# One kv head's output weights per layer as groups of 24 rows in a two-layer decode kernel

## The chip, the cores and the metric

The kernel runs on one core of a Trainium2 chip. The metric is the device time of one execution in microseconds. A run of the program takes 2570.9 us (median of three).

## The reference

Two layers of a decoder are applied twice to one token for each of two sequences: attention over a cache of 32,768 keys with 8 kv heads of 4 query heads each, then a gated feed-forward block. Both layers read the same caches and the same weights.

```
def _A_ref(x, k_cache, v_cache, wq, wo):         # B=2, D=512, Hq=32, Hkv=8, Sk=32768, Dh=128
    q = (x @ wq).reshape(B, 1, Hq, Dh)
    scores = einsum("bhqd,bhkd->bhqk", q, k) * Dh ** -0.5
    o = einsum("bhqk,bhkd->bhqd", softmax(scores), v)
    return o.reshape(B, 1, Hq * Dh) @ wo
def _B_ref(x, w_gate, w_up, w_down):             # 512 -> 1792 -> 512
    return (gelu(x @ w_gate) * (x @ w_up)) @ w_down

x = x + _A_ref(layernorm(x), ...)
x = x + _B_ref(layernorm(x), ...)
x = x + _A_ref(layernorm(x), ...)
x = x + _B_ref(layernorm(x), ...)
```

All values are float32. The output projection `wo` has 4096 rows of 512: 512 rows (1 MB) for each kv head, 128 for each of its 4 query heads.

## The kernel before

**Work and order.** A layer works through 16 pairs of a kv head and a sequence. For each pair it loads the keys in two pieces of 4 MB ([128 partitions x 16,384 numbers]) and the values in two such pieces. `scores` (L414) multiplies the keys, `softmax` follows, `values` (L485) multiplies the values, and `combine` (L494 to L503) brings the head's output `oT` into the form [128 rows of a head, 4 heads, 2 sequences]. After the second sequence of a kv head, `project` adds the head's share of the output projection to `W`, one bank of PSUM, in four groups of partitions. Layer 1 takes the pairs in the reverse order, so that the last keys and values of layer 0 are still there.

**Memory and queue.** All large data lie in one tile, `mem`, of 109 units of 512 numbers on each partition. A list, `stream`, has all loads in the order in which they are wanted. `pump` takes the next load when there is a hole of its size (a big piece has a slot of 32 units) and issues it on the SP queue (L199). `done` gives a slot back after the last product that reads it, and calls `pump` again; a load into it waits on SP until those products have run. Loads of 128 rows use 8 rows a DMA engine.

**The narrow loads.** For one kv head in each layer, (layer 0, head 6) and (layer 1, head 1), part of the output weights is stored in another form. `NARROW` has the number of query heads that are so stored: 2 in layer 0, 3 in layer 1. Their rows are cut into groups of 16 (`NROW`), and the groups lie beside each other on partitions 0 to 15, 8 groups (`NSEL`) for each query head. `pump` loads them in four transfers of four rows (L197): transfer i takes the partitions i, i+4, i+8 and i+12. They have a slot of 32 units to themselves. The other query heads of that kv head come in one more load of 128 rows, `("wo", l, g)`.

```
for i in range(4):
    nc.sync.dma_start(mem[i:NROW:4, c:c + cols], src[i])
```

**Projecting from the narrow form.** `narrow` needs the head's output in the same form. Eight small products with slices of the identity (L511) move the 16-row groups of `oT` to partitions 0 to 15 of a PSUM bank, one copy (L514) brings them to SBUF, and one product for each group and head (L519) adds to `W`. `project` then does the heads that were loaded wide (L529).

Of the kernel before, what the change touches and what calls it, by code (L numbers as in the profile page):

```python
# [16 lines left out]
P = 128  # L17
NB = 2
HKV = 8
REP = 4  # L20
DM = 512
# [6 lines left out]
HALF = 2048  # L28
# [31 lines left out]
WO_GROUPS = [[(0, 1), (2, 3), (4, 5), (6,), (7,)], [(7,), (6,), (5, 4), (3, 2), (1,), (0,)]]  # L60


NARROW = {(0, HKV - 2): 2, (1, 1): 3}
NROW = 16
NSEL = P // NROW


def pieces(split):

    out, s = [], 0  # L70
    for n in split:
        out.append((s, n))
        s += n
    return out


def parts(kind, l, pair):

    if kind == "k":
        return K_PARTS[l].get(pair, pieces(PLAIN))  # L80
    return pieces(V_SPLIT[l].get(pair, PLAIN))
# [51 lines left out]


@with_exitstack
def block_kernel(ctx: ExitStack, tc: tile.TileContext, x, consts, kt, vt, wq, wo, won, gu, wd, out):
    nc = tc.nc
    cp = ctx.enter_context(tc.tile_pool(name="cp", bufs=1))
    wk = ctx.enter_context(tc.tile_pool(name="wk", bufs=2))
# [4 lines left out]
    mem = cp.tile([P, UNITS * UNIT], F32, name="mem")  # L144
    holes = [(0, UNITS)]
    at = {}
# [3 lines left out]
    def take(key, n):  # L150
        if key in planned:
            o = planned[key]
            if not any(s <= o and o + n <= e for s, e in holes):
                return None
        elif n == CHUNK:
            spots = [o for o in range(0, UNITS - CHUNK + 1, CHUNK)
                     if any(s <= o and o + n <= e for s, e in holes)]
            if not spots:
                return None
            o = spots[0]  # L160
        else:
            fit = [(e - s, -s, e) for s, e in holes if e - s >= n]
            if not fit:
                return None
            size, s, e = min(fit)
            o = -s
        for i, (s, e) in enumerate(holes):
            if s <= o and o + n <= e:
                holes[i:i + 1] = [(x, y) for x, y in ((s, o), (o + n, e)) if y > x]
                return o  # L170
        return None

    def give(o, n):
        holes.append((o, o + n))
        holes.sort()
        i = 0
        while i + 1 < len(holes):
            if holes[i][1] == holes[i + 1][0]:
                holes[i:i + 2] = [(holes[i][0], holes[i + 1][1])]
            else:  # L180
                i += 1

    def pump():
        while stream:
            key, src, rows, cols = stream[0]
            n = CHUNK if rows == NROW else cols / UNIT if key in planned else -(-cols // UNIT)
            o = take(key, n)
            if o is None:
                return
            stream.popleft()  # L190
            c = int(o * UNIT)
            at[key] = (o, n), mem[:rows, c:c + cols]
            if rows == NROW:


                for i in range(4):
                    nc.sync.dma_start(mem[i:NROW:4, c:c + cols], src[i])  # L197
            else:
                nc.sync.dma_start(at[key][1], src)  # L199

    def flat_of(key):
        if key not in at:
            pump()
        return at[key][1]

    def get(key, a):
        return flat_of(key).rearrange("p (a c) -> p a c", a=int(a))

    def done(key, s=0, n=None):

        o, size = at[key][0]
        n = size if n is None else n
        if s + n == size:
            del at[key]
        give(o + s, n)
        pump()
# [3 lines left out]
    def flat(src, g, b, s, n):  # L220
        h, c = divmod(s, CHUNK)
        return src[b, g, h, :, c * UNIT:(c + n) * UNIT]

    def add(key, src, rows, cols):
        stream.append((key, src, rows, cols))

    def meets(l, n):

        return (l == 0 and n == len(ORDER) - 1), (l == 1 and n == 0)

    def wo_group(l, g):
        return next(t for t in WO_GROUPS[l] if g in t)

    for l in range(2):
        for i, (s, m) in enumerate(pieces(WQ_SPLIT[l])):
            add(("wq", l, i), wq[:, s * DM:(s + m) * DM], P, m * DM)
        for n, (g, b) in enumerate(orders[l]):
            second = meets(l, n)[1]
            vp = parts("v", l, (g, b))
            for s, m in parts("k", l, (g, b)):  # L240
                add(("k", l, g, b, s), flat(kt, g, b, s, m), P, m * UNIT)
            for s, m in [] if second else vp:
                if n % 2 == 1 and s == vp[1][0] and not meets(l, n)[0]:
                    group = wo_group(l, g)
                    o = g % 2 * HALF
                    if (l, g) in NARROW:
                        h = NARROW[l, g]
                        add(("won", l, g), won[l, :, :, :h * NSEL * DM], NROW, h * NSEL * DM)
                        add(("wo", l, g), wo[g // 2, :, o + h * DM:o + HALF], P, (REP - h) * DM)
                    elif len(group) == 2 and g == group[0]:  # L250
                        add(("wo", l, g), wo[g // 2], P, 2 * HALF)
                    elif len(group) == 1:
                        add(("wo", l, g), wo[g // 2, :, o:o + HALF], P, HALF)
                add(("v", l, g, b, s), flat(vt, g, b, s, m), P, m * UNIT)
            if meets(l, n)[0]:

                add(("wo", l, g), wo[g // 2, :, g % 2 * HALF:(g % 2 + 1) * HALF], P, HALF)
        for e in range(2):
            half_of = gu[e * P * FH:(e + 1) * P * FH].rearrange("(p c) -> p c", p=P)
            for j, (c, m) in enumerate(pieces(GU_SPLIT[l])):  # L260
                add(("gu", l, len(GU_SPLIT[l]) * e + j), half_of[:, c:c + m], P, m)
        for j, (o, m) in enumerate(pieces(WD_SPLIT[l])):
            add(("wd", l, j), wd[:, o * DM:(o + m) * DM], P, m * DM)
# [15 lines left out]
    nc.scalar.dma_start(xT, x)  # L279
    nc.scalar.dma_start(cst, consts)  # L280
    pump()
    ident = cst[:, C_ID:C_ID + P]

# [27 lines left out]
    def tiny(name):  # L311
        if name in once:
            return once[name]
        twice[name].reverse()
        return twice[name][1]
# [4 lines left out]
    W = ps.tile([P, 512], F32, name="W")  # L320
# [5 lines left out]
    def big():  # L326
        return wk.tile([P, 512], F32, name="big")[:, :]
# [9 lines left out]
    def small():  # L337

        u = 0 if state["full"] else state["next"]
        state["next"] = 1 - u  # L340
        return M[u]
# [163 lines left out]
    def narrow(l, g, oT, final):  # L505

        m = small()
        heads = NARROW[l, g]
        n = heads * NB
        for j in range(NSEL):  # L510
            nc.tensor.matmul(m[:NROW, n * j:n * j + n], ident[:, NROW * j:NROW * j + NROW],  # L511
                             oT[:, :heads, :].rearrange("p t b -> p (t b)"), start=True, stop=True)
        on = big()[:NROW, :NSEL * n]
        nc.vector.tensor_copy(on, m[:NROW, :NSEL * n])  # L514
        w = get(("won", l, g), NSEL * heads)
        for i in range(NSEL * heads):
            q = i % 4
            j, t = i % NSEL, i // NSEL
            nc.tensor.matmul(W[32 * q:32 * q + NB, :], on[:, n * j + NB * t:n * j + NB * t + NB], w[:, i, :],  # L519
                             start=False, stop=(final and q < heads and i + 4 >= NSEL * heads))  # L520
        done(("won", l, g))

    def project(l, g, oT, first, final):
        if (l, g) in NARROW:
            narrow(l, g, oT, final)
            h = NARROW[l, g]
            w = get(("wo", l, g), REP - h)
            for t in range(h, REP):
                nc.tensor.matmul(W[32 * t:32 * t + NB, :], oT[:, t, :], w[:, t - h, :], start=False, stop=final)  # L529
            done(("wo", l, g))  # L530
            return
        group = wo_group(l, g)
        key = "wo", l, group[0]
        w = get(key, REP * len(group))
        o = REP * (g - min(group))
        for t in range(REP):
            nc.tensor.matmul(W[32 * t:32 * t + NB, :], oT[:, t, :], w[:, o + t, :], start=first, stop=final)  # L537
        if g == group[-1]:
            done(key)
# [127 lines left out]
    for l in range(2):  # L667
        queries(l)
        stage(l, 0)
        for n, (g, b) in enumerate(orders[l]):  # L670
            if n % 2 == 0:
                oT = tiny("oT")
            p, linv = softmax(*scores(l, n, g, b))
# [16 lines left out]
    assert not stream  # L690


_INS = ["x", "consts", "kt", "vt", "wq", "wo", "won", "gu", "wd"]


def groups(x):
# [50 lines left out]
```

## Time and profile before

| | |
|---|---|
| median of 3 runs | 2570.9 us (2570.72 to 2571.05) |
| span of the profiled execution | 2568.7 us; its time outside the span is not recorded |
| PE busy | 1374.8 us (54%) |
| DVE, ACT, POOL busy | 143.6, 81.4, 2.4 us |
| DMA | 1104.81 MB, mean 430 GB/s |
| narrow loads | 4 of 128 KB (layer 0), 4 of 192 KB (layer 1) |
| wide rest of the same kv heads | 512 KB (layer 0), 256 KB (layer 1) |

The span runs from the first to the last instruction of the profiled execution. In rows of PE, "x" counts the instructions recorded; a float32 product is recorded as two. The DMA share of a stretch is the mean busy share of the core's 16 DMA engines; packets are booked where they start, so in a short stretch it may be a few hundredths too high or too low. PEclk is the granted share of the TensorE clock.

### The profile page before, as it was taken

The page shows a single profiled execution, that of the slowest core. Times are in us where ns is not written, and L with a number is a line of the kernel's source. Part 1 is how long each engine was busy: PE and PEld are TensorE (multiplying, and loading weights), DVE is VectorE, ACT ScalarE, POOL GpSimd, SP SyncE. Part 2 cuts the span into 40 slices and gives each one's busy share as a digit, 9 for nine tenths or more (in the row PEclk, how much of TensorE's full clock was granted, in tenths as well). Part 3 has the DMA queues.
Part 4 walks back from the last instruction along what each step waited for, and adds up shares of the span by engine and source line. Part 5 has one row for each costly group of instructions (what it writes and reads, how often), then busy time and mean ns, then how long its engine had stood idle before and what let it go on. Part 6 is the DMA issues. An engine that isn't in the chain of part 4 may idle for free.

```text
span 2568.7 us, 20340 instructions
## 1 busy us (share of the span) xinstructions
PE 1374.8 (54%) x9526; PEld 369.8 (14%) x9526; DVE 143.6 (6%) x483; ACT 81.4 (3%) x188; POOL 2.4 (0%) x8
## 2 busy tenths in 40 slices
PE   3545555545544554564686554454555544554657
PEld 1111111111111111111121111111111111111112
DVE  0000000000000000000011000000000000000001
ACT  0000000000000000000000000000000000000000
POOL 0000000000000000000000000000000000000000
PEclk8777777777777777777798677677776777777779
DMA  9999999999999999999999999999999999999998
GB/s 425 429 434 434 428 437 431 432 433 434 429 438 428 435 433 431 434 431 432 424 410 438 429 433 434 430 433 435 431 434 432 431 435 431 433 433 430 431 432 371
DMA packets 27507, 1104.81 MB, mean 430 GB/s; under 512 B 3200, under 2 KB 3456, under 8 KB 6912
## 3 DMA queue, kind: packets, MB, share of 16 engines
q1 hardware_dynamic: 27136, 1103.44, 99.6%
q8 instruction: 74, 1.21, 0.2%
q10 hardware_dynamic: 288, 0.08, 0.0%
q14 instruction: 9, 0.07, 0.0%
HBM read 1103.45 MB, written 0.07 MB: 430 GB/s over the span
## 4 chain that ended last, share of the span: by engine, by line
DMA 69%; PE 22%; another core or an unknown queue 8%; DVE 1%; issue 0%; ACT 0%; SPq 0%; POOL 0%; ACTq 0%; DVEq 0%
DMA mem<-in_vt 41%; DMA mem<-in_kt 24%; PE A L485 11%; PE S L414 9%; DMA aux<-in_consts 2%; DMA mem<-in_gu 1%; DMA mem<-in_wq 1%; DMA mem<-in_wd 0%; PE W L537 0%; PE M L498 0%; ACT big L494 0%; PE T L460 0%; PE W L519 0%; PE W L559 0%
## 5 line engine op out<-in xcount | busy, mean ns | idle before, releaser
L414 PE MATMUL S<-mem,aux 128*32 128x512 f32 x4032 | 575.5, 734 | 527.1 <-DMA mem<-in_kt 526.7
L485 PE MATMUL A<-mem,big 128*16 128x512 f32 x4096 | 584.7, 734 | 480.8 <-DMA mem<-in_vt 480.8
L414 PEld LDWEIGHTS S<-mem,aux 128*32 128x32 f32 x4032 | 144.9, 132 | 945.3 <-issue 508.2
L485 PEld LDWEIGHTS A<-mem,big 128*16 128x16 f32 x4096 | 122.6, 113 | 913.5 <-DMA mem<-in_vt 514.9
L417 DVE TENSOR_REDUCE aux<-S 128x1 f32<-128x512 f32 x63 | 43.6, 691 | 1110.1 <-PE S L414 1110.1
L457 ACT ACTIVATE big<-S,aux 128x512 f32<-128x512 f32 x63 | 42.7, 683 | 1187.1 <-DVE aux L453 1187.1
L460 PE MATMUL T<-aux,big 128*128 128x128 f32 x256 | 50.2, 342 | 39.0 <-ACT big L457 38.7
L503 DVE TENSOR_REDUCE aux<-M 128x4 f32<-128x64 f32 x32 | 7.2, 225 | 1103.4 <-PE M L498 1103.4
L494 ACT ACTIVATE big<-A,aux 128x512 f32<-128x512 f32 (+1 forms) x34 | 22.3, 661 | 1149.0 <-PE A L485 1149.0
L461 DVE COPY big<-T 128x512 f32<-128x512 f32 x64 | 43.8, 691 | 59.8 <-PE T L460 59.8
L460 PEld LDWEIGHTS T<-aux,big 128*128 128x128 f32 x256 | 35.8, 172 | 49.7 <-ACT big L457 49.5
L498 PE MATMUL M<-aux,big 128*128 128x128 f32 x128 | 21.3, 287 | 24.9 <-ACT big L494 24.9
L465 PE MATMUL M<-aux 128*128 128x4 f32 x64 | 17.2, 339 | 29.4 <-DVE aux L463 29.4
L449 PE MATMUL M<-aux 128*128 128x128 f32 x32 | 10.3, 323 | 34.5 <-DVE aux L447 34.5
L373 PE MATMUL M<-mem,aux 128*32 128x512 f32 x128 | 20.6, 690 | 4.4 <-DMA mem<-in_wq 3.9
L498 PEld LDWEIGHTS M<-aux,big 128*128 128x128 f32 x128 | 13.4, 140 | 53.2 <-ACT big L494 53.2
L465 PEld LDWEIGHTS M<-aux 128*128 128x128 f32 x64 | 14.4, 280 | 39.1 <-DVE aux L463 39.1
L537 PE MATMUL W<-mem,aux 128*2 128x512 f32 x96 | 12.5, 592 | 3.8 <-DVE aux L503 3.8
L333 PE MATMUL A<-aux 128*128 128x256 f32 (+2 forms) x42 | 14.3, 421 | 0.3 <-DVE aux L350 0.3
L449 PEld LDWEIGHTS M<-aux 128*128 128x128 f32 x32 | 4.2, 133 | 63.6 <-DVE aux L447 63.6
L359 PE MATMUL M<-aux 128*128 128x8 f32 x2 | 0.6, 356 | 23.2 <-DMA aux<-in_x 23.2
L457 ACT ACTIVATION_READ_ACCUMULATOR big<-S,aux 128x1 f32 x63 | 12.3, 196 | 0.0
(102 smaller groups left out, 188.8 us busy)
## 6 DMA issues: line engine op xcount, KB each, us to landing
mem<-in_gu SPq DMA_DIRECT2D x16, 896.0 KB, 24.5
mem<-in_wo SPq DMA_DIRECT2D x5, 2048.0 KB, 53.5
mem<-in_vt SPq DMA_DIRECT2D x2, 4096.0 KB, 42.2
mem<-in_kt SPq DMA_DIRECT2D x1, 7168.0 KB
mem<-in_wq SPq DMA_DIRECT2D x6, 1024.0 KB, 8.2
mem<-in_kt SPq DMA_DIRECT2D x1, 6144.0 KB
mem<-in_kt SPq DMA_DIRECT2D x5, 1024.0 KB, 8.7
mem<-in_kt SPq DMA_DIRECT2D x1, 4352.0 KB
```

The source lines that it names most:

```text
L333: nc.tensor.matmul(bank, ident[:, :bank.shape[0]], part.to_broadcast([P, n]), start=True, stop=True)
L373: nc.tensor.matmul(qp[32 * t:32 * t + 32, :], window(k, v), w[:, i - s, :], start=(i < 4), stop=(i >= 8 * KC - 4))
L414: nc.tensor.matmul(banks[u][32 * t:32 * t + 32, :], pad[:, PAD_Q - 4 * c:PAD_Q + 32 - 4 * c], w[:, j - s, :], start=(j == tile_of[0]), sto ...
L417: nc.vector.tensor_reduce(mx[:, u:u + 1], banks[u], axis=AX.X, op=OP.max)
L449: nc.tensor.transpose(m[:, :P], nm.to_broadcast([P, P]), ident)
L457: nc.scalar.activation(p[u], banks[u], AF.Exp, bias=bias, scale=SCALE, accum_out=ls[:, u:u + 1])
L460: nc.tensor.transpose(T[u][:, k * P:(k + 1) * P], p[u][:, k * P:(k + 1) * P], ident)
L461: nc.vector.tensor_copy(p[u], T[u])
L465: nc.tensor.matmul(m[:, :REP], both.to_broadcast([P, P]), same, start=True, stop=True)
L485: nc.tensor.matmul(A[32 * t:32 * t + 16, :], p[u][:, at_p:at_p + 16], w[:, QUAD * i + t, :], start=(j == 0), stop=(j == NU // QUAD - 1))
L494: nc.scalar.activation(md[:, i:i + 512 // n], A[:, i:i + 512 // n], AF.Copy, scale=linv)
L498: nc.tensor.transpose(m[:, c * P:(c + 1) * P], md[:, c * P:(c + 1) * P], ident)
```

## The change

Both kv heads' output weights are now stored narrow as a whole: all four query heads, in groups of 24 rows, 5 groups a head, on partitions 0 to 23. They come in four transfers of six rows of 40 KB (partitions i, i+4, ... i+20). Of each head's 128 rows, 5 x 24 = 120 are so covered; the last 8 rows of the four heads, 32 rows in all, come in one transfer of 32 rows of 2 KB, beside the others in the same slot. The loads of 128 rows for these two kv heads are gone.

In `narrow`, five products with slices of the identity select the groups, and four accumulating products with a zero-padded piece of the identity (`edge`, made by a memset and a copy) put the four heads' last 8 rows on partitions 0 to 31. Two copies bring both to SBUF. Then 20 narrow products and one with the 32 rest rows add to `W`.

```diff
-NARROW = {(0, HKV - 2): 2, (1, 1): 3}
-NROW = 16
+NARROW = [(0, HKV - 2), (1, 1)]
+NROW = 24
 NSEL = P // NROW
+NREST = P - NSEL * NROW
+NCOLS = REP * NSEL
+REST_Q = (REP - 1) * NREST
...
                 for i in range(4):
                     nc.sync.dma_start(mem[i:NROW:4, c:c + cols], src[i])
+                rest = mem[:REP * NREST, c + cols:c + cols + DM]
+                nc.sync.dma_start(rest, wor[key[1]])
+                at[key] += (rest,)
...
                     if (l, g) in NARROW:
-                        h = NARROW[l, g]
-                        add(("won", l, g), won[l, :, :, :h * NSEL * DM], NROW, h * NSEL * DM)
-                        add(("wo", l, g), wo[g // 2, :, o + h * DM:o + HALF], P, (REP - h) * DM)
+                        add(("won", l, g), won[l], NROW, NCOLS * DM)
...
     def narrow(l, g, oT, final):
         m = small()
-        heads = NARROW[l, g]
-        n = heads * NB
+        n = REP * NB
+        on = big()
+        edge = on[:, 64:64 + 2 * REST_Q + NREST]
+        nc.vector.memset(edge, 0.0)
+        nc.vector.tensor_copy(edge[:, REST_Q:REST_Q + NREST], ident[:, NSEL * NROW:])
+        heads = oT.rearrange("p t b -> p (t b)")
         for j in range(NSEL):
-            nc.tensor.matmul(m[:NROW, n * j:n * j + n], ident[:, NROW * j:NROW * j + NROW],
-                             oT[:, :heads, :].rearrange("p t b -> p (t b)"), start=True, stop=True)
-        on = big()[:NROW, :NSEL * n]
-        nc.vector.tensor_copy(on, m[:NROW, :NSEL * n])
-        w = get(("won", l, g), NSEL * heads)
-        for i in range(NSEL * heads):
+            nc.tensor.matmul(m[:NROW, n * j:n * j + n], ident[:, NROW * j:NROW * j + NROW], heads, start=True, stop=True)
+        k = REP * NREST
+        for t in range(REP):
+            c = REST_Q - NREST * t
+            nc.tensor.matmul(m[:k, n * NSEL:n * NSEL + NB], edge[:, c:c + k], oT[:, t, :],
+                             start=(t == 0), stop=(t == REP - 1))
+        nc.vector.tensor_copy(on[:NROW, :NSEL * n], m[:NROW, :NSEL * n])
+        nc.vector.tensor_copy(on[:k, NSEL * n:NSEL * n + NB], m[:k, n * NSEL:n * NSEL + NB])
+        w = get(("won", l, g), NCOLS)
+        for i in range(NCOLS):
             q = i % 4
-            j, t = i % NSEL, i // NSEL
-            nc.tensor.matmul(W[32 * q:32 * q + NB, :], on[:, n * j + NB * t:n * j + NB * t + NB], w[:, i, :],
-                             start=False, stop=(final and q < heads and i + 4 >= NSEL * heads))
+            t, j = divmod(i, NSEL)
+            nc.tensor.matmul(W[32 * q:32 * q + NB, :], on[:NROW, n * j + NB * t:n * j + NB * t + NB], w[:, i, :],
+                             start=False, stop=(final and 0 < q and i + 4 >= NCOLS))
+        nc.tensor.matmul(W[:NB, :], on[:k, NSEL * n:NSEL * n + NB], at["won", l, g][2], start=False, stop=final)
         done(("won", l, g))

     def project(l, g, oT, first, final):
         if (l, g) in NARROW:
             narrow(l, g, oT, final)
-            h = NARROW[l, g]
-            w = get(("wo", l, g), REP - h)
-            for t in range(h, REP):
-                nc.tensor.matmul(W[32 * t:32 * t + NB, :], oT[:, t, :], w[:, t - h, :], start=False, stop=final)
-            done(("wo", l, g))
             return
```

The weights are laid out for this on the host (`won`, and the new `wor` for the 32 rest rows).

More of the change, by code (lines that the diff above doesn't have):

```diff
@@ L135, in block_kernel @@
 @with_exitstack
-def block_kernel(ctx: ExitStack, tc: tile.TileContext, x, consts, kt, vt, wq, wo, won, gu, wd, out):
+def block_kernel(ctx: ExitStack, tc: tile.TileContext, x, consts, kt, vt, wq, wo, won, wor, gu, wd, out):
     nc = tc.nc
@@ L690, in block_kernel @@
     assert not stream
-_INS = ["x", "consts", "kt", "vt", "wq", "wo", "won", "gu", "wd"]
+_INS = ["x", "consts", "kt", "vt", "wq", "wo", "won", "wor", "gu", "wd"]
 def groups(x):
@@ L730 @@
         "wo": f(np.asarray(A_wo).reshape(HKV // 2, 2 * REP, P, DM).transpose(0, 2, 1, 3)).reshape(HKV // 2, P, 2 * HALF),
-        "won": f(np.asarray(A_wo).reshape(HKV, REP, NSEL, 4, 4, DM)[[g for _, g in NARROW]]
-                 .transpose(0, 4, 3, 1, 2, 5)).reshape(len(NARROW), 4, 4, REP * NSEL * DM),
+        "won": f(np.asarray(A_wo).reshape(HKV, REP, P, DM)[[g for _, g in NARROW], :, :NSEL * NROW]
+                 .reshape(len(NARROW), REP, NSEL, NROW // 4, 4, DM).transpose(0, 4, 3, 1, 2, 5))
+        .reshape(len(NARROW), 4, NROW // 4, NCOLS * DM),
+        "wor": f(np.asarray(A_wo).reshape(HKV, REP, P, DM)[[g for _, g in NARROW], :, NSEL * NROW:])
+        .reshape(len(NARROW), REP * NREST, DM),
         "gu": halves(np.asarray(B_w_gate), np.asarray(B_w_up)),
```

## The prediction

> **What bounds the kernel now.** I read the head of the page first, then the DMA queues, the chain, what PE waits for, and last the busy time in chosen stretches, because the change moves bytes between DMA engines and little else.
>
> ```profile
> span 2568.7 us, 20340 instructions
> DMA packets 27507, 1104.81 MB, mean 430 GB/s; under 512 B 3200, under 2 KB 3456, under 8 KB 6912
> q1 hardware_dynamic: 27136, 1103.44, 99.6%
> q8 instruction: 74, 1.21, 0.2%
> q10 hardware_dynamic: 288, 0.08, 0.0%
> DMA 69%; PE 22%; another core or an unknown queue 8%; DVE 1%; issue 0%; ACT 0%; SPq 0%; POOL 0%; ACTq 0%; DVEq 0%
> PE S L414 <- DMA mem<-in_kt: 526.7, 59, 11.2
> PE A L485 <- DMA mem<-in_vt: 480.8, 65, 15.7
> ```
>
> The data queue q1 holds the 16 DMA engines for 99.6% of the span: the kernel is one long load. PE waits for keys 59 times, 526.7 us in all, and for values 65 times, 480.8 us: about 8 us of slack at each tile. PE's 22% of the chain lies between a landing and the issue that it frees, with other tiles already queued behind; what counts is whether any DMA engine runs dry. The span is 2568.7 us; the runs' median is 2570.9, so 2.2 us lie around the span, which I keep. (The profiled execution has no other time of its own.)
>
> A transfer is done when its last engine is done, so the question is which engines are last. The stretches answer by their DMA share, where one sixteenth, 0.06, is one engine:
>
> ```profile
> core 0: us, PE busy (x) PEld busy (x) DVE busy (x) ACT busy (x) POOL busy (x), PEclk, DMA share, GB/s
> 800.00:1075.00 275.00, 136.80 (x933) 36.25 (x929) 12.13 (x40) 7.09 (x16) 0.00 (x0) 0.73 1.00 433
> 1284.00:1300.00 16.00, 11.62 (x102) 4.36 (x102) 2.70 (x14) 2.19 (x6) 0.55 (x1) 1.00 0.94 378
> 1286.50:1287.50 1.00, 0.82 (x7) 0.48 (x6) 0.00 (x0) 0.67 (x2) 0.00 (x0) 1.00 0.77 320
> 1287.50:1288.50 1.00, 0.91 (x24) 0.70 (x26) 0.30 (x2) 0.00 (x0) 0.00 (x0) 1.00 0.72 301
> 1288.50:1289.50 1.00, 0.95 (x22) 0.52 (x13) 0.00 (x0) 0.37 (x2) 0.00 (x0) 1.00 0.79 330
> 2557.00:2562.00 5.00, 4.00 (x28) 0.88 (x20) 1.99 (x5) 0.98 (x2) 0.00 (x0) 1.00 0.75 312
> 2562.00:2563.00 1.00, 1.00 (x6) 0.30 (x2) 0.00 (x0) 0.52 (x1) 0.00 (x0) 1.00 0.51 201
> 2563.00:2564.00 1.00, 1.00 (x26) 0.59 (x28) 0.00 (x0) 0.07 (x1) 0.00 (x0) 1.00 0.21 84
> 2564.00:2565.00 1.00, 1.00 (x47) 0.90 (x40) 0.00 (x0) 0.00 (x0) 0.00 (x0) 1.00 0.10 37
> 2565.00:2566.00 1.00, 0.70 (x20) 0.14 (x12) 0.16 (x1) 0.00 (x0) 0.00 (x0) 1.00 0.00 0
> ```
>
> In mid-stream all 16 are busy and move 433 GB/s, 27.1 KB/us each. At the change of layers (1286.5 to 1289.5) the share is 0.72 to 0.79: four engines have nothing left. From 2557 to 2562 it is 0.75: again four are done, some 5 us before the others, which drop out from 2562 on, one or two of them lasting until about 2565. So four engines are ahead of twelve at the end of each layer, and the last one or two set the end. A reason stands in the page: 74 instruction fetches take 0.2% of 16 engines' span, 0.002 x 16 x 2568.7 = 82 us of engine time, and engines without fetches get ahead.
>
> **Which engines a narrow transfer uses.** The count of small packets tells it.
>
> ```profile
> L197 SPq DMA_DIRECT2D mem<-in_won x8: 576/577/724, 1075.9 to 2330.1; - x8
> L199 SPq DMA_DIRECT2D mem<-in_kt x73: 327/328/457, 1.2 to 2448.9; - x73
> L199 SPq DMA_DIRECT2D mem<-in_vt x68: 327/328/426, 35.7 to 2485.4; - x68
> L199 SPq DMA_DIRECT2D mem<-in_gu x16: 327/328/429, 1263.2 to 2539.2; - x16
> L199 SPq DMA_DIRECT2D mem<-in_wo x11: 328/426/440, 111.2 to 2469.2; - x11
> L199 SPq DMA_DIRECT2D mem<-in_wq x10: 327/328/397, 0.7 to 1326.1; - x10
> L199 SPq DMA_DIRECT2D mem<-in_wd x9: 327/328/328, 1299.7 to 2550.1; - x9
> mem<-in_won SPq DMA_DIRECT2D x4, 192.0 KB
> mem<-in_won SPq DMA_DIRECT2D x4, 128.0 KB
> mem<-in_wo SPq DMA_DIRECT2D x1, 512.0 KB
> mem<-in_wo SPq DMA_DIRECT2D x1, 256.0 KB, 31.5
> ```
>
> The 288 packets of q10 are two transfers of 128 rows and 16 closing packets each. Of the 3200 packets under 512 B, 128 are the rows of x and 32 the closings on q10; 3040 remain for SP. Its 187 wide loads and the store of the result close on 16 engines each, 188 x 16 = 3008. That leaves 32 for eight narrow transfers: four each, one a row. So a four-row transfer runs on four engines, and a six-row one should run on six, closing with 48 packets; the two rest transfers stand for the two wide ones that go. After the change the count should be 3216.
>
> I call the four laden engines A, the two that six rows add B, the other ten C, and take A to stay among the six.
>
> [...]
>
> **Bytes per engine.** At 27.1 KB/us (433 GB/s over 16), in thousands of bytes, with 1 KB of the page being 1024 bytes:
> - Layer 0 before: an engine of A has four rows of 32 KB, 131.1 or 4.84 us, and every engine 32 KB of the 512 KB wide piece, 32.8 or 1.21 us.
> - Layer 1 before: A has four rows of 48 KB, 196.6 or 7.26 us, and every engine 16.4 or 0.60 us of the 256 KB piece.
> - After, in each layer: the six have four rows of 40 KB, 163.8 or 6.05 us, and every engine two rows of 2 KB of the rest, 4.1 or 0.15 us.
>
> So in layer 0 A gets 6.05 + 0.15 - 4.84 - 1.21 = +0.15 us, B +4.99, C -1.06. In layer 1 A gets -1.66, B +5.60, C -0.45. Over both, A and C lose 1.51 us and B gains 10.59. The sum of bytes stays, so the time can only come from who is last.
>
> **If B is two of the four early engines** (my forecast), B's load falls into their idle time: 3 us or more at the change of layers (idle from 1286.5, new work only after 1289.5) and 5 to 8 us at the end (2557 against 2562 to 2565). In layer 0 I take the last to be a fetching engine of C: gain 1.06 us, passed on whole, as the twelve never run dry there. If A were last, it would be a loss of 0.15; if B's lead were only the 3 us seen, B would be last by 2.0. In layer 1 A holds 7.26 us of narrow rows against 4.84 in layer 0, so the one or two that last to 2565 are most likely of A and get 1.66 us back, until C, which stops about 1 to 2 us sooner and gets back 0.45, is last instead. I take 0.9, between 0.45 and 1.66. Sum: 1.06 + 0.9 = 2.0 us; the bounds are 2.0 - 0.45 = 1.6 us slower and 1.06 + 1.66 = 2.7 us faster. The work after the last feed-forward weights follows the same engines and moves with them. 2570.9 - 2.0 = 2568.9.
>
> **What else changes, at nothing.**
>
> ```profile
> 1139.87 0.56 PE L511 MATMUL M<-aux 128*16 128x4 f32 x16 [0.32 <-DVE aux L503]
> 1140.46 0.18 DVE L514 COPY big<-M 16x32 f32<-16x32 f32 x1 [0.65 <-PE M L511]
> 1140.70 4.29 PE L519 MATMUL W<-mem,big 16*2 16x512 f32 x32 [0.27 <-DVE big L514]
> 1144.92 1.87 PE L529 MATMUL W<-mem,aux 128*2 128x512 f32 x4
> 2393.44 7.75 PE L519 MATMUL W<-mem,big 16*2 16x512 f32 x48 [0.29 <-DVE big L514]
> L300 DVE MEMSET aux<- 128x162 f32 x1 | 0.2, 193 | 0.0
> ```
>
> PE now selects with 8 products (16 records, 0.56 us) and works off 16 or 24 narrow columns (32 or 48 records, 4.29 or 7.75 us) and two or one wide ones. After: 5 + 4 selecting products, 18 records at 0.035, 0.63 us; 20 columns, 40 records at 0.134 to 0.161, 5.4 to 6.5 us; one rest column, 0.27 (two records at 0.134) to 1.87 us (all of L529). Layer 0: 0.56 + 4.29 + 1.87 = 6.7 becomes 6.3 to 9.0 us; layer 1: 48 records become 40, 1.3 us less at 0.161. DVE gets a memset (under the 0.19 us of the 128 x 162 one) and two more copies at 0.18 each, about 0.5 us; the second copy holds the first narrow product. Behind these on PE stand the next tile's scores, and SP waits for them to free space; both have the 8 us a tile of slack above, and transfers queue two deep. Without that cover it is -0.4 to +2.3 us in layer 0 and about -1 in layer 1. SP issues five transfers as before, in the same place; six rows against four at 0.58 us is within 0.1 us. The next value tile in that slot waits for five landings instead of four, all older than PE's reading of them, which it already waits for.
>
> **Rivals.**
> (1) *B is not among the four early engines, but carries fetches like the rest.* Then B gets 10.59 us on top of a full load: it would have ended between 2562 and 2565 and now ends between 2572.6 and 2575.6, against 2565: +7.6 to +10.6 us, 2578.5 to 2581.5, say 2579.9; it decides from the point where B's lead is under about 8 us. One such engine of the two is enough. If layer 0's share is partly taken up at the change of layers, it is 5.6 - 0.5 = +5.1 or more, 2576. For it: nothing in any view names an engine, and of twelve engines outside A four are early, so two picked at random are both early in 6 of 66 pairs. Against it: A was picked as the lowest rows and must have been ahead too, or its 12 us of narrow rows would have shown as a lone straggler much longer than 2 us; engines that share a burden are likely neighbours; and following the packet record of the trace from each packet's end to the next one's start, the fetches take turns on a fixed set of engines, and those without them are mostly the first to start at the launch, A among these. That speaks for B being free of fetches, though not surely.
> (2) *Six rows do not give six engines.* With three engines, two rows of every transfer each, it is 12.1 us a layer and 0.15 for the rest, against A's 6.05 and 7.86 before: +6.2, of which about 1 falls into A's distance from the last, and +4.4, so 2580.5. With rows split over all 16, every engine has 65.5, 2.42 us, against C's 1.21 and 0.60: +1.2 and up to +1.8, at most 2573.9. The count of four for four rows speaks against both.
> (3) *Much faster.* The idle engine time at the two ends is bounded: 16 x 0.06 x 16 = 15 us at 1284 to 1300, 16 x 0.25 x 5 = 20 at 2557 to 2562 and 16 x (0.49 + 0.79 + 0.90) = 35 from 2562 to 2565. All of it shared evenly gives 70 / 16 = 4.4 us, 0.17%, so a gain over 0.2% is nearly excluded.
>
> [...]
>
> **How the numbers follow.** Forecast case 0.69: 2568.2 to 2572.5 by its bounds, likeliest 2568.9. Rival 1 has 0.24; rival 2 has 0.04 with three engines and 0.01 with all 16; rival 3 has 0.02. A difference of 0.2% is 5.1 us, about what a measurement of this kernel can tell from no change: the forecast's 2.0 us, 0.08%, lies within it. So same 0.70, slower 0.28, faster 0.02. The range must reach into rival 1: from 2567.5 (the bound of 2.7 us, with a little for the clock's spread between runs) to 2580.0, its middle, which leaves out about 0.17.
>
> **What would show it.** Right: 3216 packets under 512 B; narrow issues of 240 KB; the DMA share at 1286.5 to 1289.5 up from 0.75 to nearer 0.9 (two engines idle, not four); at the end two engines out early instead of four, and the last out 2 us sooner. Wrong by rival 1: a share that falls towards 0.1 for several microseconds at the end of each layer, two engines working alone, and waits for values of 5 us more after each narrow transfer. Wrong by rival 2: another count of small packets. If PE's waits shrink by the amount the time grows, my cover for PE was gone.

## The result and the profile after

The changed kernel takes 2580.2 us (median of five runs, 2580.12 to 2580.45), the kernel before 2570.9 beside it (2570.72 to 2571.05): 9.3 us more, a ratio of 1.0036 with a 95% interval of 1.0024 to 1.0048. The forecast was 2568.9 and its range ended at 2580.0. Rival 1 had said 2579.9.

From the page of the changed kernel, its waits and its DMA issues:

```profile
span 2578.4 us, 20354 instructions
DMA packets 27347, 1104.81 MB, mean 428 GB/s; under 512 B 3216, under 2 KB 3472, under 8 KB 6736
q1 hardware_dynamic: 26976, 1103.44, 99.3%
q8 instruction: 74, 1.21, 0.2%
PE S L418 <- DMA mem<-in_kt: 531.2, 59, 12.0
PE A L489 <- DMA mem<-in_vt: 489.1, 66, 16.4
mem<-in_won SPq DMA_DIRECT2D x8, 240.0 KB
mem<-in_wor SPq DMA_DIRECT2D x2, 64.0 KB, 37.4
```

The bytes are the same, the fetches too (74). The small packets are 3216, as worked out for six engines. PE's waits for keys and values went from 1007.5 to 1020.3 us in all: PE waits longer, so PE is not where the time went. The DMA engines are busy for 99.3% instead of 99.6%: some of them stand idle longer. The stretches of the changed kernel at the change of layers and at the end say where (columns as before; 0.06 in the DMA share is one engine):

```profile
core 0: us, PE busy (x) PEld busy (x) DVE busy (x) ACT busy (x) POOL busy (x), PEclk, DMA share, GB/s
1289.00:1290.00 1.00, 1.00 (x7) 0.30 (x2) 0.00 (x0) 0.00 (x0) 0.00 (x0) 1.00 0.96 397
1290.00:1291.00 1.00, 0.61 (x5) 0.13 (x8) 0.00 (x0) 0.00 (x0) 0.00 (x0) 1.00 0.80 334
1291.00:1292.00 1.00, 1.00 (x10) 0.30 (x2) 0.00 (x0) 0.22 (x1) 0.00 (x0) 1.00 0.51 211
1292.00:1293.00 1.00, 0.82 (x7) 0.53 (x6) 0.00 (x0) 0.62 (x2) 0.00 (x0) 1.00 0.24 101
1293.00:1294.00 1.00, 0.91 (x27) 0.69 (x29) 0.30 (x2) 0.00 (x0) 0.00 (x0) 1.00 0.09 36
1294.00:1295.00 1.00, 0.91 (x22) 0.49 (x10) 0.00 (x0) 0.37 (x2) 0.00 (x0) 1.00 0.14 45
2557.00:2562.00 5.00, 2.84 (x25) 0.55 (x24) 1.57 (x4) 0.98 (x2) 0.00 (x0) 1.00 1.02 424
2564.00:2566.00 2.00, 1.48 (x10) 0.33 (x10) 0.00 (x0) 0.00 (x0) 0.00 (x0) 1.00 0.99 402
2566.00:2568.00 2.00, 1.48 (x10) 0.33 (x10) 0.04 (x1) 0.47 (x1) 0.00 (x0) 1.00 0.69 273
2568.00:2570.00 2.00, 1.20 (x8) 0.30 (x9) 1.53 (x4) 0.51 (x1) 0.00 (x0) 1.00 0.23 91
2570.00:2572.00 2.00, 2.00 (x12) 0.41 (x11) 0.42 (x1) 0.00 (x0) 0.00 (x0) 1.00 0.07 29
2572.00:2574.00 2.00, 2.00 (x42) 1.18 (x42) 0.00 (x0) 0.60 (x1) 0.00 (x0) 1.00 0.06 24
```

At the change of layers the kernel before had a share of 0.72 to 0.79 and then went on. Now the share falls through 0.80, 0.51 and 0.24 to 0.09 and 0.14. The end of the stream falls through 0.69 and 0.23 to 0.07 and 0.06: from 2570 to 2574 a single engine works and fifteen have nothing left. That is rival 1's picture, with one lone engine where it had named two. Its other sign is there too: PE's wait for the values that are queued behind the narrow rows is longer. These are the products that end it in layer 0, before and after (start, length and, in brackets, the wait ahead of it in us):

```profile
1128.87 9.21 PE L485 MATMUL A<-mem,big 128*16 128x512 f32 x64 [11.51 <-DMA mem<-in_vt]
1133.95 8.98 PE L489 MATMUL A<-mem,big 128*16 128x512 f32 x64 [15.76 <-DMA mem<-in_vt]
```

The wait grew by 4.3 us.

### The profile page after: what moved, and what is told of

Its sections match the earlier page's. It is cut to its first block, busy times and chain, and to the rows that moved or that the text cites. A ratio compares the mean times of both kernels' runs of the same rounds, so it can differ in the third digit from the quotient of the medians.

```text
span 2578.4 us, 20354 instructions
## 1 busy us (share of the span) xinstructions
PE 1371.2 (53%) x9528; PEld 372.0 (14%) x9528; DVE 144.4 (6%) x489; ACT 81.4 (3%) x188; POOL 2.4 (0%) x8
## 2 busy tenths in 40 slices
DMA packets 27347, 1104.81 MB, mean 428 GB/s; under 512 B 3216, under 2 KB 3472, under 8 KB 6736
## 3 DMA queue, kind: packets, MB, share of 16 engines
q1 hardware_dynamic: 26976, 1103.44, 99.3%
q8 instruction: 74, 1.21, 0.2%
## 4 chain that ended last, share of the span: by engine, by line
DMA 69%; PE 22%; another core or an unknown queue 8%; DVE 1%; ACT 0%; issue 0%; SPq 0%; POOL 0%; ACTq 0%; DVEq 0%
DMA mem<-in_vt 45%; DMA mem<-in_kt 20%; PE A L489 12%; PE S L418 8%; DMA aux<-in_consts 2%; DMA mem<-in_gu 1%; DMA mem<-in_wq 1%; DMA mem<-in_wd 0%; PE W L545 0%; PE M L502 0%; ACT big L498 0%; PE W L531 0%; PE T L464 0%; PE A L418 0%
## 5 line engine op out<-in xcount | busy, mean ns | idle before, releaser
L531 PE MATMUL W<-mem,big 24*2 24x512 f32 x80 | 13.3, 825 | 0.6 <-DVE big L525 0.6
```

## The experiments

**Theory 1**: some of the 16 DMA engines carry no instruction fetches and run ahead; the four laden engines and one of the two added ones are among them, the other added one carries fetches, and its bytes now set the end of both layers. **Theory 2**: the layout itself (more partitions, the rest transfer, one slot of five transfers) costs the time, whichever engines carry it. The test kernels are written like the changed one, with three numbers for each of the two narrow kv heads: rows of a transfer (so engines), transfers, and query heads in the narrow form. The changed kernel is (6, 4, 4) twice; the kernel before is (4, 4, 2) and (4, 4, 3). A diff of `NARROW` with three numbers shows how a test kernel differs from the changed one. The kernel before, run beside them, gave 2570.8 to 2570.9 us. The brackets behind a ratio are its 95% interval, about 0.1% or 2.5 us either way in most runs, so a difference of one or two microseconds is an indication and no more.

**Five rows instead of six, whole heads.**

```diff
-NARROW = {(0, HKV - 2): (6, 4, 4), (1, 1): (6, 4, 4)}
+NARROW = {(0, HKV - 2): (5, 4, 4), (1, 1): (5, 4, 4)}
```

> Both heads stored whole in groups of 20 rows, four transfers of five rows: five DMA engines with 196.6 thousand bytes each per layer (7.26 us) instead of six with 163.8 (6.05). Theory 1 (of the two engines that six rows add, one carries instruction fetches like the ten others and is last alone): if it is the sixth engine, five rows leave it out; the four get +1.4 us in layer 0 and -0.45 in layer 1 against the kernel before, so 2571.2 us (2570 to 2573). If it is the fifth, it now has 2.4 us more over both layers than with six rows: 2582.5 us. Theory 2 (the layout costs it: the rest transfer, the selecting products, the extra copies): as with six rows, 2579 to 2581 us.

Measured: 2572.8 us, ratio 1.0009 [0.9999, 1.0018]. One engine less takes away 7.4 of the 9.3 us, though five engines now carry the bytes of six and the layout is of the same kind (six groups of 20 rows a head in place of five of 24). Theory 2 falls. The time is 1.6 us above the middle that theory 1 gave, inside its range. Stretches of this kernel:

```profile
1286.00:1290.00 4.00, 3.73 (x50) 2.10 (x50) 0.30 (x2) 0.95 (x3) 0.00 (x0) 1.00 0.84 351
2560.00:2562.00 2.00, 1.13 (x7) 0.13 (x6) 1.50 (x4) 0.73 (x2) 0.00 (x0) 1.00 0.80 332
2564.00:2566.00 2.00, 2.00 (x30) 0.90 (x30) 0.00 (x0) 0.60 (x1) 0.00 (x0) 1.00 0.10 39
```

A share of 0.80 to 0.84 is 13 engines, three out early. With four rows it was four (0.75). So the fifth engine was an early one, and it has been put to use. With six rows no such step is left (0.96, 0.80, 0.51, 0.24 at the change of layers) and one engine stays at work alone: the sixth was not an early one.

**Eight rows.** No rest is left over; two more engines get rows.

```diff
-NARROW = {(0, HKV - 2): (6, 4, 4), (1, 1): (6, 4, 4)}
+NARROW = {(0, HKV - 2): (8, 4, 4), (1, 1): (8, 4, 4)}
```

> Both heads stored whole in groups of 32 rows, four transfers of eight rows: eight DMA engines with 131.1 thousand bytes each per layer (4.84 us), no rest rows, 16 columns. Theory 1: the added engines that carry fetches get 4.84 - 1.21 = 3.6 us in layer 0 and 4.84 - 0.60 = 4.2 in layer 1, 7.9 instead of 10.6 with six rows, so 2.7 us under the six-row kernel: 2577.5 us. Theory 2: no rest transfer, no padded identity, fewer products, so near or below the kernel before: 2569 to 2572 us.

Measured: 2576.5 us, ratio 1.0023 [1.0014, 1.0033], 1.0 below theory 1's middle. More partitions and fewer bytes an engine: faster than six rows by 3.7 us, as bytes on the sixth engine would have it. Two stretches of its end:

```profile
2566.00:2568.00 2.00, 1.44 (x9) 0.47 (x4) 1.23 (x4) 0.51 (x1) 0.00 (x0) 1.00 0.14 57
2568.00:2570.00 2.00, 2.00 (x11) 0.40 (x10) 0.20 (x1) 0.36 (x1) 0.00 (x0) 1.00 0.15 57
```

Here two engines (0.14, 0.15) last alone, not one: of the seventh and the eighth, one more carries fetches, by the share.

The packet records of the traces show the same directly. In mid-stream a packet starts 3 or 4 ns before the booked end of the packet ahead of it on its engine (14 or so behind a fetch), so the packets string into 16 chains, one for each engine. I take some 290 us around the narrow rows of layer 0 (840 to 1125; 830 to 1120 with five rows), a stretch in which few ends coincide. Each of these four traces has eight chains with one fetch of q8 each there and eight with none. (A packet of q14, 8 KB and 0.3 us, in the traces of four and of six rows on a laden chain, is not counted.) With four rows a transfer none of the four laden chains has a fetch; with five, none of the five; with six, one of the six; with eight, two of the eight.

**Only layer 0 changed.**

```diff
-NARROW = {(0, HKV - 2): (6, 4, 4), (1, 1): (6, 4, 4)}
+NARROW = {(0, HKV - 2): (6, 4, 4), (1, 1): (4, 4, 3)}
```

> The change in layer 0 alone; layer 1 as in the kernel before. Theory 1: the one late engine costs its 4.99 us less its distance from the last engine in layer 0, and layer 1 adds nothing: 2574.5 us (2573 to 2576). Theory 2: about half of the 9.3 us too, 2575.5. If the loss arises in layer 1 alone (the narrow rows there stand close to the end): 2570 us.

Measured: 2576.2 us, ratio 1.0019 [1.001, 1.0029]. Layer 0 costs 5.4 us (2.6 to 7.5 by the interval), which leaves about 4.0 for layer 1. Stretches of this kernel at the two ends:

```profile
1292.00:1293.00 1.00, 0.82 (x6) 0.57 (x6) 0.00 (x0) 0.58 (x2) 0.00 (x0) 1.00 0.24 101
1293.00:1294.00 1.00, 0.91 (x27) 0.70 (x29) 0.30 (x2) 0.00 (x0) 0.00 (x0) 1.00 0.11 43
2564.00:2566.00 2.00, 1.23 (x8) 0.33 (x9) 1.51 (x4) 0.51 (x1) 0.00 (x0) 1.00 0.76 317
2566.00:2568.00 2.00, 2.00 (x12) 0.38 (x11) 0.42 (x1) 0.00 (x0) 0.00 (x0) 1.00 0.73 302
```

The lone engine stands at the change of layers alone; the end has the kernel before's 0.75 again, 5 us later.

**Six rows with half the load.** Two query heads narrow, two wide, in both layers.

```diff
-NARROW = {(0, HKV - 2): (6, 4, 4), (1, 1): (6, 4, 4)}
+NARROW = {(0, HKV - 2): (6, 4, 2), (1, 1): (6, 4, 2)}
```

> The changed kernel's transfers of six rows in both layers, but with two of the four query heads in the narrow form (rows of 20 KB instead of 40 KB), the other two as a load of 128 rows. Theory 1 (one of the two added engines carries instruction fetches, and its bytes set the end of both layers): it gets 81.9 + 32.8 + 2.0 = 116.8 thousand bytes a layer instead of 167.9, 1.89 us less at 27.1 KB/us, in each of two layers: 2580.2 - 3.8 = 2576.4, between 2575.5 and 2577.5. Theory 2 (six rows on 24 partitions cost a fixed time, whatever their length): 2579.5 to 2580.5.

Measured: 2576.0 us, ratio 1.002 [1.0011, 1.0029]. The time follows the bytes on the added engine: 4.2 us less for 3.8 worked out. A fixed price of six rows is out.

**No narrow loads at all.**

```diff
-NARROW = {(0, HKV - 2): 2, (1, 1): 3}
+NARROW = {}
```

> No narrow loads: both kv heads' output weights as loads of 128 rows like all the others. Every engine gets 65.5 thousand bytes a layer. Theory 1: the twelve get 32.8 (layer 0) and 49.2 (layer 1) more, 1.2 and 1.8 us: 2570.8 + 3.0 = 2573.8 where one of the twelve was last in both layers; 2572 where a laden engine was last in layer 1, which loses 5.4 us of load. Eight engines, not four, should then be out early at the end of a layer: a DMA share near 0.5 for some microseconds.

Measured: 2573.5 us, ratio 1.0011 [1.0002, 1.0021]. Stretches of this kernel:

```profile
1288.00:1289.00 1.00, 0.86 (x6) 0.67 (x6) 0.02 (x1) 0.45 (x2) 0.00 (x0) 1.00 0.57 238
1289.00:1290.00 1.00, 0.91 (x30) 0.71 (x32) 0.28 (x2) 0.00 (x0) 0.00 (x0) 1.00 0.50 208
1290.00:1291.00 1.00, 0.90 (x16) 0.49 (x8) 0.00 (x0) 0.37 (x2) 0.00 (x0) 1.00 0.52 215
2560.00:2562.00 2.00, 1.54 (x11) 0.16 (x7) 1.14 (x3) 0.93 (x2) 0.00 (x0) 1.00 0.53 222
2562.00:2564.00 2.00, 1.47 (x11) 0.58 (x12) 0.85 (x2) 0.05 (x1) 0.00 (x0) 1.00 0.50 207
```

With equal loads, half the engines are done early: eight of 16, for some 3 us at the change of layers and at least 4 at the end. So the order is: eight early with no narrow load, four with four rows, three with five.

**More instructions, no more data.** Is it the instruction fetches that the other eight carry?

```diff
+    def extra(bank, n):
+        for _ in range(28 if 0 < n < len(ORDER) - 2 else 0):
+            nc.tensor.matmul(bank[:16, :REP], ident[:, :16], same, start=True, stop=True)
...
         m = small()
+        extra(m, n)
         nc.tensor.transpose(m[:, :P], nm.to_broadcast([P, P]), ident)
```

(The same call stands ahead of the sum's product in `softmax` and of the transposes in `combine`.)

> The kernel before with 2184 small products more on TensorE (28 before each of three products of a pair, of 16 x 4 results each, in 26 of the 32 pairs, written over by the product behind them), so more instructions to fetch and no more data: 8736 instructions, where 20340 go with 74 + 9 fetches, about 34 fetches more. Theory 1 (eight of the 16 engines carry the fetches, those without them get ahead by as much, and the others set the end): 34 fetches at 1.1 us (82 us over 74) over eight engines, +4.7 us, 2575.5, between 2573.5 and 2578; the share of 0.75 before the end of a layer lasts longer by 2 to 3 us. Theory 5 (the lead of the early engines has nothing to do with fetches): the products stand in the slack of 8 us a tile, 2 us each, 2570.5 to 2571.5.

Measured: 2576.6 us, ratio 1.0023 [1.0013, 1.0032]. From its page and its stretches:

```profile
span 2574.7 us, 29076 instructions
q8 instruction: 108, 1.77, 0.3%
2564.00:2566.00 2.00, 1.22 (x7) 0.13 (x6) 1.41 (x4) 0.82 (x2) 0.00 (x0) 1.00 0.75 312
2566.00:2568.00 2.00, 1.79 (x12) 0.58 (x12) 0.58 (x2) 0.00 (x0) 0.00 (x0) 1.00 0.56 233
2568.00:2570.00 2.00, 2.00 (x30) 0.81 (x26) 0.00 (x0) 0.60 (x1) 0.00 (x0) 1.00 0.44 175
```

34 fetches more (108 for 74), 0.56 MB, cost 5.6 us: over eight engines 4.25 each, 1.3 us apiece where 1.1 was worked out. In the packet records the 108 fetches took 115.2 us together and the 74 before 79.0, which is 4.5 us more for each of eight engines; what the last 1.1 us are is not shown. The stretch of 0.75 did not get longer, as was expected. In its place the share falls on to about a half (0.56, 0.44) towards the end, as it would if the lead had outgrown what the four laden ones carry. Theory 5 falls: the lead comes from fetches. In mid-stream (800 to 1075 us) the share is 1.00, so the products hid in PE's slack. The 8736 instructions more stand against 34 fetches more, 257 apiece: PE has the slack for them, but this kernel, which its DMA engines bound, pays 5.6 us for the fetches.

**Six transfers of four rows** (groups of 24 rows, but on four engines, partitions i, i+6, i+12, i+18).

```diff
-NARROW = {(0, HKV - 2): (6, 4, 4), (1, 1): (6, 4, 4)}
+NARROW = {(0, HKV - 2): (4, 6, 4), (1, 1): (4, 6, 4)}
```

> The six-row kernel's layout (groups of 24 rows, 32 rest rows, the same products and copies), but loaded by six transfers of four rows: four DMA engines with 245.8 thousand bytes each per layer (9.07 us). Theory 1: the fifth and sixth engine are relieved; the four get 9.07 + 0.15 - 6.05 = +3.2 us in layer 0 and +1.4 in layer 1 against the kernel before, of which about 1 falls into their distance from the last in layer 0: 2574.5 us (2572.5 to 2575.5). Theory 2: the layout is as it was, 2579 to 2581 us.

Measured: 2592.5 us, ratio 1.0083 [1.0066, 1.0099]. Both theories missed it by over 11 us. Two things could be behind it: four engines with 246 thousand bytes each, or the step of six. With a step of four, and if the kth row goes to the kth engine, each engine writes to a group of four partitions of its own (4k to 4k+3); with a step of six, neighbours write into one another's group. Two kernels tell these apart.

**The kernel before with the rows of a transfer on adjacent partitions.**

```diff
-                    nc.sync.dma_start(mem[i:rows:parts_n, c:c + cols], src[i])
+                    nc.sync.dma_start(mem[r * i:r * i + r, c:c + cols], src[i])
```

> The kernel before, but each transfer of four rows goes to four adjacent partitions instead of every fourth one: the same bytes on the same four engines, with four engines writing into adjacent partitions at once. Theory 3 (the six transfers of four rows with their step of six lost time because several engines wrote into the partitions of one another): slower than before by some us to tens of us, 2574 to 2600. Theory 4 (they lost it because four engines with 246 thousand bytes each are overladen): nothing changes, 2570.8, between 2570.3 and 2571.5.

Measured: 2583.0 us, ratio 1.0049 [1.0034, 1.0064]. Apart from the partitions only the order of the rows in DRAM has changed, so that each partition gets the numbers that it had, and 12.1 us are lost. By the packet records the 16 narrow rows of 32 KB in layer 0 took 1.91 us each in the median and 3.07 at most, where all took 1.21 to 1.22 before; the 16 rows of 48 KB in layer 1 took 3.35 in the median, before 1.82. The load of 128 rows behind the narrow one in layer 1 lands 42.3 us after its issue, where it was 31.5 in the kernel before:

```profile
mem<-in_wo SPq DMA_DIRECT2D x1, 256.0 KB, 42.3
```

**Four engines with more bytes, each on its own partitions.**

```diff
-NARROW = {(0, HKV - 2): (6, 4, 4), (1, 1): (6, 4, 4)}
+NARROW = {(0, HKV - 2): (4, 4, 4), (1, 1): (4, 4, 4)}
```

> The kernel before, but with all four query heads narrow in both layers: the 16-row groups and transfers of four rows of 64 KB to every fourth partition, no wide rest. The four engines get 262.1 thousand bytes a layer, 9.68 us, against 6.05 (layer 0) and 7.86 (layer 1): more than in the kernel with six transfers of four rows (245.8 and 4.1), but each engine writes to its own partitions. Theory 3 (the partitions): +1.8 to +5 us, 2572.5 to 2576. Theory 4 (four overladen engines): like the six transfers of four rows, 2591 to 2595.

Measured: 2576.4 us, ratio 1.0023 [1.0013, 1.0032], just above theory 3's upper end. So 262 thousand bytes on each of four engines cost 5.6 us and not 22: theory 4 falls, and the partitions are shown to matter. The four engines of the six transfers are not the only ones to pay: around the narrow rows of that trace (1085 to 1150 and 2340 to 2420 us) 70 of 815 packets of 64 KB took over 3 us, where in the changed kernel 4 of 910 did and the median is 2.42. How the other 16 us come about in full stays open, and no run shows what makes the adjacent rows 12.1 us slower.

**A version that might beat both:** five engines, with the loads adjusted to their lead.

```diff
-NARROW = {(0, HKV - 2): (6, 4, 4), (1, 1): (6, 4, 4)}
+NARROW = {(0, HKV - 2): (5, 4, 3), (1, 1): (5, 4, 4)}
```

> Groups of 20 rows in transfers of five rows, with three query heads narrow in layer 0 and four in layer 1: five engines that are all early by theory 1 get 122.9 + 16.4 thousand bytes (layer 0) and 163.8 (layer 1), beside a rest load, and the others 16.4 less than before in each layer. Theory 1: a little faster than the kernel before, 2570.0, between 2569.5 and 2571.5, less than a measurement can tell. Theory 2 (narrow rows on more than 16 partitions cost a fixed time): 2572.5 or more, like the whole heads in transfers of five rows (2572.8).

Measured: 2571.6 us, ratio 1.0003 [0.9994, 1.0011]: no difference that can be told from the kernel before, and 1.6 us more than worked out. No version here beats the kernel before.

## Why the prediction was wrong

- *The bound* was right: DMA engines, and the last of them. In the kernel before, a load of 128 rows has eight packets and a closing one on each of 16 chains, and the products on the keys at 1069.29 us started 0.13 us after the last of its 16 closings had landed. The time came from idle engines at the two ends of layers, with the same bytes and mid-stream rate (433 GB/s from 800 to 1075 us before and after).
- *Six rows use six engines*: right (3216 small packets, on the number, and six chains). Rival 2 is out. The number alone does not set the time: with whole heads narrow, five engines took 2572.8 us, six 2580.2 and eight 2576.5. It hangs on which engines the rows go to.
- *B is two of the four early engines*: this is the step that failed. One of the two is early, the other carries fetches: with five rows 2572.8, with six 2580.2, and one fetch on one of the six chains. I had followed the packet records of the kernel before, and rightly found that the fetches take turns on a fixed set of engines, but only its four laden engines can be told by their rows there. The four laden engines are free of q8's fetches, as I took them to be, but I went on from them to "engines that share a burden are likely neighbours", a guess that no run shows. Nor does one show that A is among the six, which the sums take for granted: the runs show how many laden chains have a fetch (none of four, none of five, one of six, two of eight), and no view names an engine. The count that stood beside it, 6 of 66 pairs, was the better guide. It could have been sharpened: if four of twelve are early, two picked at random are both early in 9%, one of them in 48% (32 of 66 pairs), and rival 1 needs no more than one fetching engine.
- *Rival 1's sum* was right: +7.6 to +10.6 us, middle 9.1, measured 9.3. By layers: layer 0 was 4.99 and measured 5.4. Layer 1 was 5.60 and measured 4.0, 1.6 less, as it would be if the engine that now ends last had ended about that much ahead of the last one before, within the 0 to 3 us I had allowed. That the total met the middle to 0.2 us is luck: nothing fixed this distance beforehand, layer 0 came out above its term and layer 1 below, and the interval of the one-layer run is wide enough for either to be chance. "One such engine of the two is enough" was the case. The range stopped at this rival's middle and so missed the result by 0.2 us; its upper end, 2581.5, was a bound of the same sum.
- *The gain of 1.06 + 0.9* for the others could not show: they no longer set the end. Five engines with adjusted loads came out 0.7 us above the kernel before, where 0.9 less was worked out, so I may have put this gain too high with early engines alone; the interval holds both signs.
- *Work on PE and DVE at nothing*: right. The timeline of the changed kernel, both narrow heads:

```profile
1144.72 0.42 PE L519 MATMUL M<-aux 128*24 128x8 f32 x10 [0.32 <-DVE aux L507]
1145.00 0.41 PE L523 MATMUL M<-aux,big 128*32 128x2 f32 x8
1145.69 6.37 PE L531 MATMUL W<-mem,big 24*2 24x512 f32 x40 [0.28 <-DVE big L525]
1151.81 1.91 PE L533 MATMUL W<-mem,big 32*2 32x512 f32 x2
2402.39 6.96 PE L531 MATMUL W<-mem,big 24*2 24x512 f32 x40 [0.28 <-DVE big L525]
```

Selecting starts at 1144.72 and ends at 1145.41, 0.7 us against the 0.63 worked out. The narrow columns took 6.37 and 6.96 against 5.4 to 6.5, the rest column 1.91 against 0.27 to 1.87, so layer 1's columns and the rest column are a little over. Layer 0's sum is 0.7 + 6.4 + 1.9 = 9.0, at the top of 6.3 to 9.0. All of it was hidden: PE's waits grew, they did not shrink by the amount that the time grew.

## What to carry to other kernels

This kernel is bound by its DMA engines (99.6% of its span), and a transfer of four, five, six or eight rows was a load on that many of its 16 engines. In such a kernel, first find how many rows go to engines that really are ahead: run the ladder of row counts, and read the idle sixteenths at the ends of stages or the chains of packets, before any sum of bytes. Where two engines must both be early, count the pairs, and trust the count over a story of neighbours. Measure where on the partitions the rows should go: in transfers of four rows here, rows four partitions apart took 2570.9 us (the kernel before) and 2576.4 (four engines with more bytes), adjacent rows 2583.0 and rows six apart 2592.5.

## What the runs showed of the hardware

- In the stretches of some 290 us that were followed, eight of the 16 DMA engines carried the instruction fetches of q8, one each, and the other eight none. 8736 TensorE instructions more raised the fetches of q8 from 74 to 108 (16 KB each, 1.07 us in the median). Of the engines that a transfer of four or five rows used none was among the eight, of those that six rows used one was, of those that eight rows used two were. The 34 fetches more cost this DMA-bound kernel 5.6 us, though TensorE itself had slack.
- Four rows of a transfer on four adjacent partitions cost 12.1 us more over two narrow heads than the same rows on every fourth partition; a row of 32 KB took 1.91 us in the median instead of 1.21 to 1.22.
